# Store and move issues regrouped at the end of an attention and spectral-mixing kernel: 64-row stores on the Sync queue, three late row moves on Sync, two more wide jobs stored block by block

## The chip, the cores and the metric

The kernel runs on one core of one Trainium2 chip. The metric is the device time of one execution in microseconds (us), as a median over runs. A profile is of one execution; its clock starts at its own first instruction. To compare profiles I measure from one landmark, the start of ScalarE's copy of `yl`, the last thing that no edit here touches, and write such times as L+x.

## The reference, cut to what matters

Causal attention with decay over 8 batches, 8 heads, 576 positions, then spectral mixing and a gated output:

```python
x = attention(q, k, v, f)                 # 8 x 576 x 512 after joining heads
X = np.fft.rfft(x, axis=1)                # 64 modes are kept
Y[:, :64] = complex_matmul(X[:, :64], w_r, w_i)   # per mode a 512 x 512 matrix
y = np.fft.irfft(Y, n=576, axis=1)
u = x + y
out = u + np.maximum(u @ w_ch, 0.0)       # 9.44 MB, float32
```

## The kernel before

For some 400 us the kernel streams weights. The change is in what follows. When the last modes are done, their inverse-transform rows are computed for all batches into `yls[0]`, and small DMAs ("moves", 16 KB each) carry each batch's rows to where TensorE needs them in `yy`. The move of batch b is written (b,0) for the plain rows and (b,1) for the rows multiplied by `w_ch`.

```python
def emit_moves(yl, r0, b, t, eng):
    p0 = H4 * b
    ins = eng.dma_start(row_slot(b, t, r0, H4), yl[p0 : p0 + H4, t, :])
    if eng is nc.gpsimd:
        tc.keep_in_program_order(ins)
...
nc.scalar.copy(yls[0][:, 0, :], ply[:, :])          # the landmark L
emit_moves(yls[0], H2, 1, 0, nc.gpsimd)
run(terms(jobs[0], ps, 0, "y"))
...
nc.vector.tensor_copy(yls[0][:, 1, :], plw[:, :])
emit_moves(yls[0], H2, 1, 1, nc.gpsimd)
for b in range(2, B):
    for t in range(2):
        emit_moves(yls[0], H2, b, t, nc.gpsimd)
```

Then 20 jobs follow. In each, TensorE makes two PSUM tiles (`pu` = u, `pz` = u times `w_ch`), ScalarE copies `pu` out, VectorE does relu and add, and Sync or ScalarE stores the block:

```python
def emit_o(job, ps, u, o, pair, split=False):
    ...                                              # VectorE: relu and add
    if sb == 4:                                      # the 64-row job of a batch pair
        for h in range(2):
            eng = (nc.sync, nc.scalar)[h]
            eng.dma_start(out[b + h, 512:576, :], o[64 * h : 64 * h + 64, 0, :])
    elif not wide(job):
        nc.sync.dma_start(...)
    elif sb % 2 or n_wide < 2:                       # wide: one store for two jobs
        rs = slice(sb % 2 if n_wide < 2 else 0, sb % 2 + 1)
        ...
```

While TensorE waits for the last weights, it is kept busy with matmuls whose results are overwritten later:

```python
def fill(n):
    for k in range(n):
        rows = slice(k % 2, k % 2 + 1)
        run(*(terms(jobs[0], ps, t, "x")[rows] for t in range(2)), pin=True)

fill(4)                                              # 16 matmuls of 512 columns
```

The softmax here doesn't subtract the row's maximum and nothing guards it: scores larger than these inputs give would overflow.

## Time and profile before

| | before |
|---|---|
| time, median of 3 runs | 437.63 us (437.60 to 438.23) |
| profiled span | 436.5 us |
| last compute ends (VectorE, job 19) | 428.16, L+26.13 |
| end of the span | L+34.47 |
| output | 9.44 MB in the last 31 us |

The sliced page shows where the change plays. Each figure stands for a fortieth of the span, so only the last three or four of each line count:

```profile
DMA  8999999999999999999999999999999999994797
GB/s 175 236 235 237 239 235 238 235 211 237 233 215 237 226 223 237 211 237 234 214 237 211 211 212 211 211 211 212 211 212 211 211 211 211 211 211 84 273 341 276
```

The weights keep the DMA engines at 0.9 until slice 36. Then there is a gap (84 GB/s), in which the late rows are made and moved, and after it the output stores. GpSimd's timeline of this gap (start, length, what; in brackets how long it was idle and what ended that):

```profile
403.21 0.51 POOL L823 DMA_DIRECT2D yy<-yl  x1 [17.51 <-ACT yl L1070]
404.15 4.30 POOL L823 DMA_DIRECT2D yy<-yl  x9 [0.42 <-DVE yl L1074]
```

GpSimd issues (1,0) at L+1.18, 0.6 us after ScalarE's copy has ended, and (1,1) at L+2.12, 0.30 us after VectorE's copy.

### The profile page before, as it was taken

Reading aid. Unit: us, or ns where it says so; the run is one execution under the profiler, and the core shown is the slowest. Engines: PE = TensorE matmul, PEld = TensorE weight load, DVE = VectorE, ACT = ScalarE, POOL = GpSimd, SP = SyncE. Lnnn points to the kernel's source line nnn. Section 1 sums busy time; section 2 is a strip of 40 time slices with the busy share of each in tenths; the row PEclk is TensorE's granted clock in tenths of the full one; section 3 lists DMA queues with packets and bytes.
Section 4 is the critical chain, followed back from the end, with each engine's and each line's share of the span. In section 5 each row is a group of like instructions: output and inputs, shape, how many; then the busy total and the mean of one; then the engine's idle time right before and its main releaser. Section 6 shows DMA issues by size and latency. Waiting matters only on the chain.

```text
span 436.5 us, 12293 instructions
## 1 busy us (share of the span) xinstructions
PE 357.7 (82%) x5295; PEld 243.4 (56%) x5313; DVE 263.8 (60%) x658; ACT 224.7 (51%) x340; POOL 128.9 (30%) x202
## 2 busy tenths in 40 slices
PE   3787798999797886877877886999979978899881
PEld 2454666776675665565655665766644544454440
DVE  5797888877565564665666677333233645553892
ACT  2887489775444636436447282233424434542670
POOL 7333332423233233232332232332223232200500
PEclk9996899998766857758759597799999999989997
DMA  8999999999999999999999999999999999994797
GB/s 175 236 235 237 239 235 238 235 211 237 233 215 237 226 223 237 211 237 234 214 237 211 211 212 211 211 211 212 211 212 211 211 211 211 211 211 84 273 341 276
DMA packets 50981, 97.37 MB, mean 223 GB/s; under 512 B 3792, under 2 KB 12976, under 8 KB 50928
## 3 DMA queue, kind: packets, MB, share of 16 engines
q0 software_dynamic: 46688, 86.16, 100.7%
q1 hardware_dynamic: 3920, 9.91, 6.3%
q8 instruction: 41, 0.67, 0.6%
q10 hardware_dynamic: 320, 0.52, 0.5%
q14 instruction: 12, 0.10, 0.1%
HBM read 163.73 MB, written 9.44 MB: 397 GB/s over the span
## 4 chain that ended last, share of the span: by engine, by line
DMA 40%; PE 26%; ACT 10%; DVE 7%; issue 4%; POOL 0%; DVEq 0%; ACTq 0%
DMA wb<-in_moe_w_i_dram 39%; ACT E L576 7%; PE pav L614 6%; PE ps L569 5%; PE A L188 5%; PE tp L307 4%; ACT KT L320 2%; DVE QTs L322 2%; PE vp L541 2%; DVE os L1005 1%; PE px L657 1%; PE pz L828 1%; ACT VT L326 1%; PE px L682 1%; DVE E L591 1%
## 5 line engine op out<-in xcount | busy, mean ns | idle before, releaser
L576 ACT ACTIVATE E<-ps 128x1024 bf16<-128x1024 f32 (+1 forms) x128 | 101.4, 851 | 21.7 <-PE ps L569 11.3
L188 PE MATMUL A<-XT,wb 128*128 128x16 bf16 x1984 | 70.4, 181 | 13.6 <-DMA wb<-in_moe_w_i_dram 8.9
L188 PEld LDWEIGHTS <-wb 128*128 128x128 bf16 x1984 | 63.7, 99 | 27.3 <-issue 11.4
L93 POOL DMA_DIRECT2D wb<-in_moe_w_r_dram x64 | 42.4, 663 | 119.6 <-DMA wb<-in_moe_w_r_dram 21.9
L569 PE MATMUL ps<-QTs,KT 64*128 64x64 bf16 (+4 forms) x384 | 56.8, 316 | 19.6 <-ACT E L576 17.7
L93 POOL DMA_DIRECT2D wb<-in_moe_w_i_dram x64 | 42.3, 661 | 87.3 <-DMA wb<-in_moe_w_i_dram 43.9
L614 PE MATMUL pav<-va,E 128*128 128x65 bf16 (+1 forms) x1088 | 53.1, 205 | 3.2 <-DVE x_all L636 2.6
L614 PEld LDWEIGHTS <-E 128*128 128x128 bf16 (+1 forms) x1088 | 43.5, 111 | 18.4 <-issue 9.3
L591 DVE TENSOR_TENSOR E<-E,trimask 128x256 bf16<-128x256 bf16 (+2 forms) x128 | 36.9, 302 | 20.5 <-ACT E L576 20.2
L867 ACT CAST XW<-pxw 128x512 bf16<-128x512 f32 x36 | 20.8, 587 | 39.4 <-PE pxw L860 34.5
L326 ACT COPY VT<-tp 128x640 bf16<-128x640 bf16 (+1 forms) x32 | 23.2, 761 | 32.4 <-PE tp L307 32.4
L569 PEld LDWEIGHTS <-KT 64*128 64x128 bf16 x384 | 18.8, 97 | 32.5 <-issue 20.9
L860 PE MATMUL pxw<-wch,yy 128*128 128x512 bf16 x133 | 35.1, 398 | 1.3 <-issue 0.5
L910 ACT CAST XW<-pB 128x512 bf16<-128x512 f32 x36 | 21.0, 586 | 27.8 <-PE pB L828 27.7
L320 ACT COPY KT<-tp 128x640 bf16<-128x640 bf16 (+1 forms) x32 | 21.9, 748 | 25.9 <-PE tp L307 25.8
L909 DVE CAST x_all<-pA 128x512 bf16<-128x512 f32 x36 | 24.9, 692 | 14.0 <-PE pA L828 12.4
L322 DVE COPY QTs<-tp 128x640 bf16<-128x640 bf16 (+1 forms) x32 | 23.4, 767 | 14.3 <-PE tp L307 14.0
L636 DVE TENSOR_TENSOR x_all<-pav,rcp 128x384 bf16<-128x384 f32 x64 | 29.1, 455 | 0.9
L153 DVE TENSOR_TENSOR YTe<-A,Yacc 128x128 bf16<-128x128 f32 x16 | 5.9, 367 | 33.1 <-PE A L188 33.1
L828 PEld LDWEIGHTS <-ident_bf 64*64 64x64 bf16 (+1 forms) x348 | 15.8, 108 | 17.9 <-issue 8.9
L625 DVE RECIPROCAL rcp<-pav 128x6 f32<-128x6 f32 x64 | 12.1, 189 | 20.0 <-PE pav L614 19.4
L860 PEld LDWEIGHTS <-yy 128*128 128x128 bf16 x144 | 12.7, 101 | 15.2 <-DVE yy L854 4.6
(143 smaller groups left out, 622.2 us busy)
## 6 DMA issues: line engine op xcount, KB each, us to landing
wb<-in_moe_w_r_dram POOLq DMA_DIRECT2D x62, 512.0 KB, 16.9
wb<-in_moe_w_i_dram POOLq DMA_DIRECT2D x62, 512.0 KB, 17.8
stv<-in_v_dram POOLq DMA_DIRECT2D x10, 576.0 KB, 15.1
out_dram<-os SPq DMA_DIRECT2D x10, 512.0 KB, 5.0
stk<-in_k_dram POOLq DMA_DIRECT2D x11, 288.0 KB, 15.3
stq<-in_q_dram POOLq DMA_DIRECT2D x11, 288.0 KB, 15.3
wx<-in_v_dram POOLq DMA_DIRECT2D x5, 576.0 KB, 15.5
out_dram<-uo SPq DMA_DIRECT2D x3, 512.0 KB, 4.0
```

Source lines behind the costliest of these rows:

```text
L93: keep(nc.gpsimd.dma_start(dst, src))
L188: ins = nc.tensor.matmul(A[:, eb, mi, :], lhsT=w_of(mi, eb * 128), rhs=x_of(m), start=(i == 0), stop=(i == len(terms) - 1),)
L320: nc.scalar.copy(rows(KTs[pr % 2][:, :, 0:S]), tv)
L322: ins = nc.vector.tensor_copy(rows(QT[pr][:, :, :]), tv)
L326: nc.scalar.copy(rows(VTs[pr % 2][:, :, 0:S]), tv)
L569: nc.tensor.matmul(ps[:, b, o : o + n], lhsT=KTs[pr % 2][bs, h, jb * 128 : (jb + 1) * 128], rhs=QT[pr][bs, h, jb * 128 + c0 : jb * 128 + c ...
L576: nc.scalar.activation(E[:, :, piece * 512 : piece * 512 + w], ps[:, :, 0:w], ACT.Exp, scale=scale,)
L591: nc.vector.tensor_tensor(dg, dg, tr, ALU.mult)
L614: nc.tensor.matmul(pav[64 * half : 64 * half + w, slot, :], lhsT=E[:, b, c : c + (w - 1) * st + 1 : st], rhs=va[:, jb, b, :], start=(n == ...
L636: nc.vector.tensor_tensor(xo, pi, ri, ALU.mult)
L860: nc.tensor.matmul(pxw[:, :], lhsT=xT[:, eb, i * 128 : (i + 1) * 128], rhs=wch[:, eb, :], start=(eb == 0), stop=(eb == NDC - 1),)
L909: nc.vector.tensor_copy(xs, pA[:, :])
```

## The change

It has three parts. (1) The moves (1,0), (2,0) and (3,0) go to Sync, to shorten GpSimd's line-up. (2) All 64-row stores but the very last go to Sync alone, so that no store issue stands in ScalarE's queue and Sync's and ScalarE's rings don't mix. (3) Jobs 7 and 8 (the second half of the first four wide jobs) are stored one by one, sooner.

```diff
-            if eng is nc.gpsimd:
+            if eng is nc.gpsimd or r0 == H2:
                 tc.keep_in_program_order(ins)
...
-                        eng = (nc.sync, nc.scalar)[h]
+                        eng = nc.scalar if job is jobs[-1] and h else nc.sync
...
-                elif sb % 2 or n_wide < 2:
-                    rs = slice(sb % 2 if n_wide < 2 else 0, sb % 2 + 1)
+                elif sb % 2 or n_wide < 4:
+                    rs = slice(sb % 2 if n_wide < 4 else 0, sb % 2 + 1)
...
-        emit_moves(yls[0], H2, 1, 0, nc.gpsimd)
+        for b in (1, 2, 3):
+            emit_moves(yls[0], H2, b, 0, nc.sync)
...
-            for t in range(2):
+            for t in range(1 if b < 4 else 0, 2):
                 emit_moves(yls[0], H2, b, t, nc.gpsimd)
```

## The prediction

> **What bounds the kernel now.** I read the sliced page first (the last three of 40 slices are the only ones above 270 GB/s), then the chain of waits, then the timelines of VectorE and Sync, half-microsecond windows, and last the DMA queues of chosen stretches. The change touches nothing before about 402.6 us, so 34 us of a 436.5 us span are in play. These last microseconds are: spectral weights end, late rows `yl` are copied by small DMAs into `yy`, then PE, ACT and DVE make 20 blocks ("jobs"; I number them 0 to 19) and 9.44 MB go out. Jobs 0-3 are of batches 0 and 1, job 4 is their 64-row job, jobs 5-8 are the wide ones of batches 2 and 3, 9 the 64-row one, and so on.
>
> The chain of waits, as pieces in order of time (start, length, what):
>
> ```profile
> 404.15 1.44 POOL yy L823 x3
> 405.58 3.76 DMA yy<-yl
> 409.35 0.04 issue
> 409.39 0.40 PE pu L828 x2
> ...
> 410.29 0.70 DVE uo L1005
> 411.00 0.02 issue
> 411.02 0.57 ACTq L1013
> 411.59 0.04 issue
> 411.63 1.02 ACT us L1000
> ```
>
> See two delays: PE waits until 409.35 for the fourth move behind GpSimd's line-up (batch 3, t=0), and a 0.57 us store issue stands in ScalarE's queue before the evacuation of job 6. The VectorE timeline shows the second delay again, and what the same spot costs in the next batch pair:
>
> ```profile
> 412.67 3.48 DVE L1005 SCALAR_TENSOR_TENSOR os<-pz,us 128x1024 f32<-128x1024 f32 x3 [0.56 <-ACT us L1000]
> ...
> 418.38 3.48 DVE L1005 SCALAR_TENSOR_TENSOR os<-pz,us 128x1024 f32<-128x1024 f32 x3 [0.21 <-ACT us L1000]
> ```
>
> But the last compute (VectorE, job 19) ends near 428.16, and the span ends at 436.5. So the bound of the end is the store traffic. Sync's timeline and the windows (length, busy of PE PEld DVE ACT POOL, clock, DMA share, GB/s):
>
> ```profile
> 425.33 4.02 SPq L1026 DMA_DIRECT2D out_dram<-os  x4
> 429.44 1.76 SPq L1013 DMA_DIRECT2D out_dram<-uo  x1
> ```
>
> ```profile
> 416.50:417.00 0.50, 0.50 (x16) 0.35 (x12) 0.32 (x2) 0.09 (x1) 0.00 (x0) 1.00 0.10 37
> 417.00:417.50 0.50, 0.50 (x16) 0.29 (x9) 0.50 (x1) 0.17 (x1) 0.00 (x0) 1.00 1.02 401
> ...
> 427.50:428.00 0.50, 0.00 (x0) 0.00 (x0) 0.50 (x2) 0.00 (x0) 0.00 (x0) 1.00 1.02 414
> ```
>
> At 416.5 the engines run dry, because job 7's block is held until job 8's is done. Adding the half-microsecond windows backwards from 435.0, the last 2.36 MB (eight 128x1024 stores and job 19) start to flow at about 427.4, 2.1 us after their first store was issued at 425.33: by then there is a backlog, and time lost earlier in the store stream is never won back. Where is it lost? The DMA queues of three stretches, 417.0 to 418.5, 418.5 to 420.5 and 424.0 to 426.0 (q1 is Sync's ring, q10 ScalarE's):
>
> ```profile
> DMA packets 162, 0.60 MB, mean 401 GB/s; under 512 B 15, under 2 KB 15, under 8 KB 162
> ```
>
> ```profile
> DMA packets 191, 0.57 MB, mean 287 GB/s; under 512 B 20, under 2 KB 20, under 8 KB 190
> q1 hardware_dynamic: 121, 0.44, 65.9%
> q10 hardware_dynamic: 69, 0.12, 31.2%
> ```
>
> ```profile
> DMA packets 205, 0.61 MB, mean 304 GB/s; under 512 B 27, under 2 KB 27, under 8 KB 205
> q1 hardware_dynamic: 135, 0.49, 68.9%
> q10 hardware_dynamic: 70, 0.12, 30.8%
> ```
>
> While ScalarE's 64-row store is mixed with Sync's stream, the engines are as busy as ever but move 287 and 304 GB/s, not 401. (In 427.5 to 430.0, q1 alone, it is 419.) Q10 holds 0.12 MB for 31% of the busy time, q1 0.44 MB for 66%: 2.6 against 1.5 per cent per 10 KB.
>
> **What the Trainium skill says.** "DMA: Bandwidth & Descriptors", section "Issuing engines are not separate DMA queues": DMAs of all issuers run on the same 16 engines and interleave, and spreading the issue saves only sequencer time. The trace agrees that they interleave, and goes further: total rate falls by about a quarter while they do. "SBUF — State Buffer", section "Door 1: The DMA port swizzle": 64 partitions reach only 8 of the 16 ports, with an asymptote near 218 GB/s. That speaks against two 64-row stores in a row on one queue; in the trace Sync's own 64-row stores sit in windows of 303 and 332 GB/s (420.5 and 427.0), mixed with other stores, so no window isolates one. "DMA: Bandwidth & Descriptors", section "Measured", has smaller transfers at lower rates; the trace disagrees where they are queued back to back: from 414.0 to 416.0 q1 alone moved 256 KB stores with 2 KB rows at 395 GB/s, 5% under the wide ones.
>
> **Part 1: three moves to Sync.** GpSimd issues 14 moves at 0.484 us each. Before, the order is (batch 1, t=0), (1,1), (2,0), (2,1), (3,0): the first at 403.21, the next from 404.15, so (3,0) is issued at 404.15 + 3 x 0.484 = 405.6 and lands at 409.35. After, (1,0), (2,0), (3,0) go to Sync as soon as ScalarE's copy of `yl` ends (402.03 + 0.59 = 402.62). Sync's earlier moves took 0.588 us each, so they are issued by 404.4; even at Sync's median of 4.6 us to landing, measured under the weight stream, (3,0) is there by 408.4. Sync's first output store was at 404.70, so it isn't delayed. GpSimd's (2,1) and (3,1) come two places earlier too, landing near 409. PE had the four x-terms of job 5 done near 408.45 and then waited; its last two y-terms began at 409.39 and now begin near 408.8. **Gain 0.6 us** for jobs 4 and 5.
>
> **Part 2: 64-row stores on Sync.** Four ACT issues become one. (a) The issue at 411.02 goes: ScalarE can begin job 6 as soon as `pu` is there, and VectorE's 0.56 us wait falls to the 0.2 or so of the later pairs. **Gain 0.35 to 0.55 us** of compute. The issues at 416.79 and 422.49 (0.49, 0.47) end before the `pu` that ScalarE then waits for; worth nothing in compute. So compute ends about 1.0 us earlier, at 427.1. (b) The mixing of rings goes for jobs 4, 9 and 14: in each of two stretches of 2 us about 2 x (401 - 295)/401 = 0.5 us was lost; at job 4 (412.5 to 413.5 at 193 and 283 GB/s, where a late issue overlaps it) perhaps as much. Against this, 0.26 MB of 64-row stores in a row at some 320 GB/s takes 0.8 us, not 0.65: 0.15 us each.
>
> **Part 3: jobs 7 and 8 one by one.** Two 512 KB stores become four of 256 KB, the first two a job earlier (job 7 ended 1.2 us before 8). That fills the dry half-microsecond at 416.5 (0.45 us). Cost: 1.05 MB in 2 KB rows, 5% of 2.6 us, 0.13 us; two more Sync issues of 0.33 to 0.5 us, hidden.
>
> **Sum, as a ledger of the store stream after the change.** The first 2.1 MB (jobs 0-3), paced by compute, flow until 412.6 as now (413.0, less the late GpSimd moves). Then job 4: 0.26 MB, 0.8 us, 413.4. Jobs 5-8: 2.1 MB at 395, 5.3 us, 418.7. Job 9: 0.8, 419.5. Jobs 10-13: 2.1 MB at 410, 5.1 us, 424.6. Job 14: 0.8, 425.4. The last 2.36 MB take 7.2 us now (427.4 to 434.6), ScalarE's last 64-row store still among them, so they end at 432.6. Can compute feed it? With everything 1.0 us earlier, jobs 10 and 11 are issued at 418.6, 12 and 13 at 420.9, 15 and 16 at 424.3: with the 0.8 us from issue to flow seen at 416.19 to 417.0, the first of these is flowing at 419.4, just in time, the others with room. 434.6 - 432.6 = **2.0 us** less: 437.63 - 2.0 = **435.6 us**, 0.5% faster.
>
> **Rivals.** (1) Compute sets the gain: the stream is no shorter, it only starts earlier, so the 1.0 us of parts 1 and 2a comes through: 436.6. For it: near-equal rates, one batch pair of 2.36 MB per 5.7 us of compute is 414 GB/s. Against: the backlog of 2.1 us at 427.4. (2) The slow stretches come from the 64 rows (8 ports), not from two rings; then two in a row on Sync are as slow or slower and the end moves by 0.5 us at most: 437.1. For it: the skill's port table; q10's cost per byte. Against: the windows 420.5 and 427.0 with Sync's own 64 rows at 303 and 332, for half a microsecond, not two. (3) Sync as the only issuer becomes the bound: its issues already stretch from 0.33 to 1.76 us late in the stream, and more stores wait for a completion eight stores back. Then the gain is lost: 437.6 or 0.3 more. Against: [...]the engines stay at 410 GB/s. (4) The moves on Sync land late behind output stores, and PE waits as before: 0.6 us less gain.
>
> **Range and chances.** The ledger gives 435.6; if both ring mixing and gap filling pay in full and the tail too, 434.8; rival 1 gives 436.6, rival 2 437.1. I hold the ledger at 0.6, rival 1 at 0.2, the others together 0.2: range 434.8 to 436.9. Two per cent is 8.75 us, more than the whole drain after the last compute: faster 0.01, slower 0.01, same 0.98.
>
> **What would show it.** Right: no DMA piece of `yy<-yl` near 409 in the chain; VectorE's wait before job 6 at 0.2 or less; its last end near 427.1; no window under 350 GB/s between 413 and 425 with q10 present; no dry window at 416.5; the last 2.36 MB starting near 425.4. Wrong: two 64-row stores on q1 in a stretch under 250 GB/s; Sync's issues beginning over 1 us after VectorE's ends while the DMA share is below 0.9; PE still waiting for a move.

## The result, and the profile after

| | before | after |
|---|---|---|
| time, median of 6 runs each, same rounds | 438.31 us (437.6 to 439.0) | 440.22 us (439.71 to 441.63) |
| ratio of the fast runs, 95% interval | | 1.0052 (1.0030 to 1.0073) |
| profiled span | 436.5 | 438.0 |
| last compute ends | L+26.13 | L+28.57 |
| end of the span | L+34.47 | L+36.50 |

A ratio is the mean time of one kernel's fast runs over that of the other's in the same rounds, so it is not quite the ratio of the medians. The kernel is 1.9 us slower, where 2.0 us faster was predicted. It is within 2%, but outside the predicted range of 434.8 to 436.9.

The chain of waits of the kernel after (start, length, what) has a DMA piece where the one of before stood. It ends at L+5.86, 1.5 us earlier than that one (L+7.32), and is almost as long:

```profile
403.52 0.47 issue
403.99 3.34 DMA yy<-yl
407.33 0.04 issue
407.37 0.64 PE pz L828 x2
...
411.11 1.24 DVE uo L1005
```

The timeline of TensorE shows the wait, and that of GpSimd the issue:

```profile
407.37 0.64 PE L828 MATMUL pz<-yy,BIl 64*64 64x512 bf16 x2 [1.89 <-DMA yy<-yl]
```

```profile
403.99 5.29 POOL L823 DMA_DIRECT2D yy<-yl  x11 [18.99 <-ACT uo L1000]
```

The late move is now (1,1), for job 2. With (1,0) gone, it is the first move that GpSimd issues, at L+2.52 instead of L+2.12, and it takes 3.34 us where it took 1.6. TensorE stands still for 1.89 us. The matmuls after it take 0.64 us where the same pair took 0.40, because the clock is halved. Half-microsecond windows (length, busy time of PE, PEld, DVE, ACT, POOL, then clock, DMA share, GB/s):

```profile
407.50:408.00 0.50, 0.50 (x8) 0.29 (x9) 0.00 (x0) 0.00 (x0) 0.50 (x2) 0.50 0.97 352
...
410.00:410.50 0.50, 0.50 (x10) 0.32 (x9) 0.18 (x1) 0.00 (x0) 0.00 (x0) 0.50 0.03 6
...
421.00:421.50 0.50, 0.15 (x4) 0.00 (x0) 0.50 (x2) 0.42 (x2) 0.00 (x0) 1.00 1.04 295
421.50:422.00 0.50, 0.47 (x10) 0.26 (x11) 0.50 (x1) 0.50 (x1) 0.00 (x0) 1.00 0.26 66
422.00:422.50 0.50, 0.50 (x12) 0.38 (x10) 0.50 (x1) 0.23 (x1) 0.00 (x0) 1.00 0.57 139
```

At 410.0 the engines have nothing to store, because compute is late. From 421.0 the 64-row pair of job 9 goes out, now on one ring. Sync takes 1.49 us (420.10 to 421.59) to issue the second store of the pair; its packets begin near 422.1, behind a dry stretch, and from 421.5 to 423.0 the engines move 150 GB/s. VectorE's timeline tells how late compute is, and that one step of the prediction came true:

```profile
408.95 1.23 DVE L1005 SCALAR_TENSOR_TENSOR uo<-pz,uo 128x1024 f32<-128x1024 f32 x1 [2.80 <-PE pu L828]
...
414.55 3.49 DVE L1005 SCALAR_TENSOR_TENSOR os<-pz,us 128x1024 f32<-128x1024 f32 x3 [0.21 <-ACT us L1000]
```

The wait before job 6 was 0.56 us and is 0.21. But VectorE lost 2.80 us before job 2. Job 5 starts at L+11.65 where it was L+8.87, 2.8 us later; compute ends 2.4 us later and the span 2.0 us later. Of these 2.0 us, 1.4 are the last store, which lands at L+34.77 (before: L+33.38). The other 0.6 us come after it: from that landing to the end of the span it is 1.73 us where it was 1.09. Sync there goes through the completion waits of the stores one after another, and 7 of them are still to come when the last store lands, where it was 4. No run isolates this.

For a stretch that holds little but a 64-row pair (112 of its 120 data packets are 2 KB rows), 428.0 to 429.0 of the kernel after, the DMA queues were:

```profile
DMA packets 153, 0.26 MB, mean 262 GB/s; under 512 B 33, under 2 KB 33, under 8 KB 153
q1 hardware_dynamic: 153, 0.26, 90.7%
```

One ring, no mixing, 0.9 busy, and still 262 GB/s. In the packet records of the kernel after, the mean 2 KB packet took 99 to 160 ns in the half-microseconds in which 64-row pairs flow on Sync's ring, and 84 to 90 ns where 128-row stores do. Not every packet is slower: in this stretch the median is 84 ns, and one in ten took over 165. (The 137 to 169 ns of an expectation below are means of the last store, on ScalarE's ring.)

### The profile page after: what moved, and what is told of

Same layout as the page of the kernel before. It is cut to its first block, busy times and chain, and to the rows that moved or that the text cites. A ratio compares the mean times of both kernels' runs of the same rounds, so it can differ in the third digit from the quotient of the medians.

```text
span 438.0 us, 12298 instructions
## 1 busy us (share of the span) xinstructions
PE 358.8 (82%) x5295; PEld 244.1 (56%) x5313; DVE 263.4 (60%) x658; ACT 224.7 (51%) x340; POOL 127.2 (29%) x199
## 4 chain that ended last, share of the span: by engine, by line
DMA 51%; PE 21%; ACT 7%; DVE 6%; issue 3%; DVEq 0%; POOL 0%; ACTq 0%; POOLq 0%
DMA wb<-in_moe_w_i_dram 43%; DMA stk<-in_k_dram 7%; ACT E L576 5%; PE pav L614 4%; PE ps L569 4%; PE A L188 3%; PE tp L307 3%; PE pz L828 2%; DVE os L1005 1%; PE px L657 1%; ACT KT L320 1%; DVE QTs L322 1%; PE px L682 1%; PE pu L828 1%; PE vp L541 1%
```

## The experiments

Fifteen variants ran, each five rounds against the kernel before; all were correct. J5 is the start of VectorE's work for job 5, C the end of compute, both in us from L and read from one profile each, so they can differ from the runs behind the ratio.

| run | ratio, 95% interval | J5 | C |
|---|---|---|---|
| (before) | | 8.87 | 26.13 |
| (after) | 1.0052 (1.0030 to 1.0073) | 11.65 | 28.57 |
| moves_only | 1.0055 (1.0026 to 1.0085) | 11.97 | 28.96 |
| no_moves | 0.9991 (0.9970 to 1.0012) | 8.68 | 25.41 |
| sync64_only | 0.9978 (0.9960 to 0.9996) | 8.95 | 25.69 |
| single_only | 0.9994 (0.9976 to 1.0011) | 9.07 | 26.33 |
| b11_sync | 1.0036 (1.0009 to 1.0063) | 12.77 | 30.68 |
| b10_pool | 0.9984 (0.9966 to 1.0002) | 8.30 | 25.22 |
| warm | 1.0043 (1.0015 to 1.0071) | 12.29 | 29.21 |
| first64 | 0.9985 (0.9965 to 1.0005) | 9.18 | 25.97 |
| after_shift48 | 0.9994 (0.9975 to 1.0012) | 9.17 | 26.09 |
| before_shift16 | 0.9998 (0.9979 to 1.0018) | 9.47 | 26.47 |
| before_shift48 | 0.9987 (0.9970 to 1.0004) | 8.30 | 25.29 |
| first64_single_b10 | 0.9980 (0.9965 to 0.9995) | 8.29 | 25.28 |
| b11_shift48 | 0.9990 (0.9974 to 1.0007) | 8.59 | 25.51 |
| b10_shift48 | 0.9992 (0.9975 to 1.0008) | 8.30 | 25.21 |
| best_shift48 | 1.0000 (0.9987 to 1.0013) | 8.29 | 25.31 |

### The parts by themselves

`moves_only` is part 1 alone, `no_moves` parts 2 and 3, `sync64_only` part 2, `single_only` part 3; each is the kernel before with those hunks of the diff, the first and the last two being part 1, the second part 2, the third part 3.

> Part 1 alone (three moves on Sync). Theory A: the loss sits here. GpSimd's first move of batch 1, t=1, now comes after a pause of 19 us and its 16 packets meet the first output stores, so it lands near 407.3 instead of 405.6, PE idles about 1.9 us and then runs at half clock: expect 1.5 to 2.8 us slower than before (ratio 1.003 to 1.006), the wait of PE for yy near 407 and the half clock both present. Theory B (the stores of parts 2 and 3 cost the time, the late move is hidden by the store backlog): within 0.5 us of before.

> Parts 2 and 3 without part 1. Theory A: the moves arrive as in the kernel before, PE doesn't idle near 407, and the gain of the dropped ScalarE issue (0.35 us) and of the filled gap (0.3 to 0.5 us) shows: 0.3 to 1.2 us faster than before. Theory B: 64-row stores in a row on one ring[...] (137 to 169 ns for a 2 KB packet in the changed kernel, 84 elsewhere): 0.5 to 2 us slower than before.

> Part 2 alone. Prediction's step 2: mixing of two rings goes (0.5 us each time), less 0.15 us each for 64 rows in a row, and compute gains 0.35: 0.8 to 1.4 us faster. From the changed kernel's packet times I now expect that the two rows of halves cost as much alone as mixed: 0 to 0.5 us faster. Theory B: slower by 0.5 us or more.

> Part 3 alone. Fills the dry half-microsecond at 416.5: if the store backlog bounds the end, 0.3 to 0.5 us faster; if compute or the pair's wait later on bounds it, within 0.2 us; the dry window should be gone in either case.

Measured: 440.37, 437.61, 437.19 and 437.96 us, against 437.85 for the kernel before. **The whole loss is in part 1**: its run has the same wait for the same move (2.08 us) and the halved clock. The other parts gain a little or nothing. Part 2 brings the end of compute forward by 0.44 us (26.13 to 25.69). Where the store stream's share went, Sync's timeline of `no_moves` shows:

```profile
419.18 1.91 SPq L1013 DMA_DIRECT2D out_dram<-uo  x2
421.18 3.19 SPq L1026 DMA_DIRECT2D out_dram<-os  x4
```

VectorE had ended job 11 at 420.15, but its store is issued at 421.18, because Sync was still issuing the two 64-row stores. The DMA engines run dry meanwhile:

```profile
420.50:421.00 0.50, 0.50 (x14) 0.29 (x10) 0.50 (x1) 0.39 (x1) 0.00 (x0) 1.00 0.08 29
```

So two store issues in a row on one queue made a hole of 0.5 us that two queues had not made.

### Who should issue which move

In `b11_sync`, (1,1) goes to Sync too; in `b10_pool`, (1,0) goes back to GpSimd, as its first move.

```diff
 # b11_sync, on the kernel after
-        emit_moves(yls[0], H2, 1, 1, nc.gpsimd)
+        emit_moves(yls[0], H2, 1, 1, nc.sync)
 # b10_pool, on the kernel after
-        for b in (1, 2, 3):
+        emit_moves(yls[0], H2, 1, 0, nc.gpsimd)
+        for b in (2, 3):
             emit_moves(yls[0], H2, b, 0, nc.sync)
```

> The changed kernel with batch 1, t=1 moved by Sync too, in one queue ahead of the output stores. Theory A (GpSimd's move behind the output stores is the loss): it lands before job 2 needs it, PE's 1.9 us wait and the half clock go: 1.5 to 2.5 us faster than the changed kernel, so 0 to 1 us faster than the kernel before. Rival (any use of Sync for moves delays the output stores, and that is the loss): still 1.5 us or more slower than before.

> The changed kernel with batch 1, t=0 given back to GpSimd, which issues it before batch 1, t=1; Sync keeps (2,0) and (3,0). If the first issue after GpSimd's pause is what lags (0.70 us behind VectorE's end in the changed kernel, 0.30 in the kernel before, where it came second), (1,1) is issued 0.4 us earlier against its inputs and lands before the stores flow: as fast as b11_sync, 0 to 1 us faster than before. If the landing is late for another reason, the wait of 1.9 us stays and it is 1.5 us or more slower than before.

`b10_pool` did as expected: no wait for (1,1), job 5 at L+8.30, 437.56 us against 437.99. `b11_sync` missed. Issued by Sync, the move was as late as in the kernel after, and TensorE stood for 2.21 us. In its profile, the slowest of its six runs, the clock then stayed halved for 10.2 us, where it was 3.4 us in the kernel after; this goes with its late C. So "GpSimd's first move is slow" could not be the whole cause.

### Does the halved clock do it?

`warm` puts 16 matmuls that add zeros into TensorE's wait, on the kernel after:

```diff
+            elif n == 2:
+                run([zs[0]], [us[0]], pin=True)
+                for _ in range(8):
+                    for p, _w, src, _f in zs[0]:
+                        tc.keep_in_program_order(add(p, BIe[1][HS[0], 0:HM], src, False))
+                run(zs[1:], us[1:], pin=True)
```

> The changed kernel with 16 matmuls of zero weights, adding nothing, in PE's wait for the move (some 1.7 us of work). The move lands as late as in the changed kernel, but PE doesn't stand still. If the half clock from 407 to 410.5 is a result of the standstill and half the damage, the clock stays full and it is 0.8 to 1.5 us faster than the changed kernel, 0.5 to 1.5 us slower than before. If the clock is halved regardless, it is as slow as the changed kernel.

Measured: 439.72 us. The move came later still (4.14 us), 1.29 us of wait were left, and the clock was halved all the same from about 409.9. This run is inconclusive: it did not separate the standstill from the clock.

`first64` keeps ScalarE's 64-row stores except for job 4 (`eng = nc.scalar if b and h else nc.sync`, on the kernel before).

> Part 2 for job 4 alone; the later 64-row stores stay split over Sync and ScalarE. From sync64_only: compute gains 0.44 us there by the dropped issue at job 4, while the later pairs on Sync hold up the next store (issue times of 3.1 and 2.5 us for two) for nothing. So 0.4 to 1.0 us faster than before, at least as fast as sync64_only. If instead the unmixing of the rings is what sync64_only gains from, about 0.2 us faster only.

Measured: 437.78 us, no different from part 2 as a whole within the intervals.

### What held up the move

A DMA counts its semaphore up to 16. The Trainium skill, "DMA: Bandwidth & Descriptors", section "Why a DMA increments its semaphore by 16 and not by 1", says that for a GpSimd DMA all 16 DMA engines post one count each, and that only the full 16 means that the data has landed. The trace's semaphore records agree, and they show what the profile's one number of 3.34 us hides. The last column is the 16,384-byte packet of the instruction queue nearest in time:

| kernel | move | issued | 15th count | 16th count | instruction packet |
|---|---|---|---|---|---|
| before | (1,1) | 404.15 | 405.75 | 405.78 | 406.83 to 407.71 |
| before | (3,0) | 405.58 | 408.03 | 409.35 | 406.83 to 407.71 |
| after | (1,1) | 403.99 | 406.30 | 407.33 | 404.95 to 406.28 |
| b11_sync | (1,1) | 404.55 | 406.41 | 408.24 | 405.46 to 406.82 |
| before_shift16 | (1,0) | 403.76 | 405.39 | 406.94 | 404.83 to 405.83 |
| after_shift48 | (1,1) | 404.53 | 406.89 | 406.92 | 401.50 to 402.57 |
| b11_shift48 | (1,1) | 404.60 | 406.43 | 406.46 | 401.61 to 402.54 |

In the kernel after, fifteen engines were done at 406.30 and the sixteenth 1.03 us later. In the stretch 404.9 to 406.3 of that kernel the view of the queues lists, beside Sync's ring and GpSimd's, one packet of a third:

```profile
q1 hardware_dynamic: 140, 0.26, 50.2%
q0 software_dynamic: 38, 0.02, 10.7%
q8 instruction: 1, 0.02, 6.0%
```

It is 16,384 bytes and took 1.33 us. The skill, "Runtime: NRT & Kernel Launch", section "Instruction fetch mechanics", says that each engine's instruction memory is refilled in blocks of 16 KiB, 256 instructions, over a DMA queue of its sequencer's own, and that the cost is "mostly hidden". The trace agrees on the block: it holds 5295 matmuls and 5313 weight loads of TensorE, 41.4 blocks of 256, and this queue carried 41 packets (42 with 48 loads and matmuls more). That it is hidden was to be tested. The runs with a shift in their names move the fetch in time and leave the moves alone: the 16 filling matmuls are cut into four (or two) of fewer columns each, which adds 48 (or 16) weight loads and as many matmuls at about the same TensorE time.

```diff
-        fill(4)
+        fill(4, 4)      # each of 512 columns as 4 of 128; before_shift16: fill(4, 2)
```

> The kernel after with 48 more weight loads and matmuls in TensorE's queue, at about the same TensorE time: the 16 filling matmuls before the last but one mode group, whose results are overwritten, are cut into four of 128 columns each. Nothing of the moves changes, only where in time the 16,384-byte instruction fetches fall (they come about every 128 weight loads; in the kernel after one ran on one DMA engine from 404.95 to 406.28, over the move of batch 1, t=1, whose last completion count came at 407.33). Theory F (the fetch holds up the move): the fetch comes some 5 us earlier, the move lands near 405.7 to 406.0, no 3 us DMA piece in the chain, the clock isn't halved, compute ends near +26 of the copy of yl, time 437.2 to 438.0, ratio to before 0.998 to 1.001. Theory O (the move is late because it is GpSimd's first and starts 0.4 us later, into the first output stores; the early fetch is only a by-product of TensorE's wait): wait and time as in the kernel after, ratio 1.004 to 1.006.

> The kernel before with 16 more weight loads and matmuls ahead, by cutting the same 16 filling matmuls in two. Its fetch, at 4.80 us after the copy of yl, should come some 16 loads sooner, near 3.4 to 3.5 us after it, when the move of batch 1, t=1 is in flight (issued 404.15, complete 405.78 in the kernel before). Theory F: that move, or one behind it, is complete 1 to 2 us later, TensorE stands, ratio to before 1.003 to 1.006; if the move's packets on that engine are through before the fetch begins, which is possible because it starts 0.4 us sooner here than after the change, only part of it, 1.001 to 1.003. Theory O: as before, 0.999 to 1.001.

> The kernel before with the 48 additional weight loads and matmuls of the first run: a control for that edit, and a look at whether the fetch also causes the late landing of batch 3, t=0 (409.35 in the kernel before, with a fetch from 406.83 to 407.71). Theory F: the 3.76 us DMA piece that ends at 409.35 shrinks to 2 to 2.5 us, compute of job 5 begins up to 0.6 us earlier, ratio 0.997 to 0.9995. Theory O: nothing moves, 0.999 to 1.001.

`after_shift48`: **the loss is gone**, 437.89 us against 438.17, where the same kernel without the edit stood at 1.0052. The fifteenth and sixteenth count are 0.03 us apart. The kernel before with the same loads stands at 0.9987, so with the fetch out of the way on both sides the change is worth nothing that these intervals show. The wait and the clock:

```profile
406.96 0.40 PE L828 MATMUL pz<-yy,BIl 64*64 64x512 bf16 x2 [0.95 <-DMA yy<-yl]
```

```profile
407.50:408.00 0.50, 0.50 (x14) 0.32 (x8) 0.11 (x1) 0.12 (x1) 0.50 (x2) 1.00 0.63 211
```

`before_shift16` makes the fault appear in the kernel before. The fetch now falls on the first move, (1,0), whose sixteenth count comes 1.55 us after the fifteenth; TensorE waits where it had not waited:

```profile
406.98 0.40 PE L828 MATMUL pu<-yy,BIl 64*64 64x512 bf16 x2 [1.04 <-DMA yy<-yl]
```

It fell one move earlier than I had aimed. The clock stayed whole, job 5 came 0.6 us later than before, and the time did not move measurably (0.9998): here only the trace speaks for theory F, the ratio lies where theory O had it. `before_shift48` takes the fetch away from all of the early moves. The DMA piece that ends at 409.35 in the kernel before disappears and job 5 starts at L+8.30: with no change to any move, it has 0.57 of the 0.6 us that part 1 was to bring.

I looked at the 17 profiles together. In the 12 without the 48 loads the fetch falls among the moves issued after L, and some move's sixteenth count comes 1.0 to 1.95 us after its fifteenth. In the five with them the fetch is over by L+0.6 and no such gap is over 0.34 us.

For the miss of `b11_sync`, and for what GpSimd's order is worth by itself, the same 48 loads were put into those two variants:

> The kernel with batch 1, t=1 on Sync as well (its run missed: 1.0036, TensorE waiting 2.21 us), now with the 48 additional weight loads that put the instruction fetch elsewhere. Theory F (that miss was the fetch too): the move, issued about 2.5 us after the copy of yl begins, lands within 1.5 to 2.4 us, TensorE waits at most 0.9 us, the clock is not halved, ratio 0.997 to 1.000. Rival (a move issued this late lands late in any case, because the output stores have begun): wait over 1.3 us, clock halved, ratio 1.003.

> The kernel after with batch 1, t=0 left as GpSimd's first move, and with the 48 additional weight loads. If the fetch costs this variant nothing (its run showed no wait at the moves, 0.9984), nothing changes: 0.997 to 1.0. If the fetch held up other moves in it (three of GpSimd's had their last count 1.6 to 1.9 us behind the fifteenth), these come sooner: 0.996 to 0.998. In both, the wait at batch 1, t=1 stays under 0.4 us, which, beside the 0.95 us of the first run with 48 more loads, is what the order of GpSimd's moves alone is worth.

The profile of `b11_shift48` has TensorE wait this long, where `b11_sync` had 2.21 us:

```profile
406.50 0.40 PE L828 MATMUL pz<-yy,BIl 64*64 64x512 bf16 x2 [0.37 <-DMA yy<-yl]
```

So that miss had the same cause. `b10_shift48` has no wait for a move at all. The 0.95 us that `after_shift48` keeps is therefore what giving up (1,0) as GpSimd's first move costs. In time it is not to be seen (0.9992 and 0.9994).

### A better version

> The parts that earlier runs showed to help, together: 64-row stores on Sync for the first of the four 64-row jobs alone, the blocks of jobs 7 and 8 one by one, batch 1, t=0 left as GpSimd's first move, and t=0 of batches 2 and 3 on Sync. If the gains add (0.9985 for the first part, 0.9994 for the second, 0.9984 for the kernel after with GpSimd's first move given back): 0.996 to 0.998, 436.1 to 437.1. Rival: the end is paced by the last 2.36 MB of stores behind a compute that ends no earlier in any of these, and the gains do not add: 0.998 to 1.000.

> The kernel with Sync's 64-row stores for the first 64-row job alone, single blocks and GpSimd's first move given back (0.998), and the 48 additional weight loads. If the gains add: 0.9965 to 0.998, 436.4 to 437.1. If the store stream sets the end whatever the compute does: as without the loads, 0.998 to 0.9995.

`first64_single_b10` is the kernel after with the edits of `first64` and `b10_pool`; `best_shift48` adds the 48 loads to it.

The first ran at 437.53 us against 438.17, ratio 0.9980: faster than the kernel before by 0.2%, and no faster than part 2 alone (0.9978). With the additional weight loads the gains did not add: 438.30 us against 437.99, ratio 1.0000, though compute ends at L+25.31, 0.8 us before that of the kernel before. In its profile the stores did not take this back: the last one landed at L+32.16, 1.2 us sooner than in the kernel before. But from there to the end of the span it is 1.86 us, where it was 1.09, and L itself came 0.4 us later, 402.45 for 402.03.

## Why the prediction was right or wrong

**Part 1, the step that failed.** The text says of GpSimd's queue only that "(2,1) and (3,1) come two places earlier too, landing near 409". It did not ask which move becomes the first, and which job needs that one. It is (1,1), whose first matmul runs at L+3.8 in the kernel before and for which TensorE stands from L+4.0 on in the kernel after; it is issued 0.4 us later and lands later. Alone that is 0.95 us of wait and nothing in the time. The rest came from what no line of the argument had: an instruction fetch that fell on this move. Shown is that moving the fetch, with the moves unchanged, takes the late sixteenth count away (in all five variants with the 48 loads) and puts it on another move in `before_shift16`. Argued only is that both sit on the same DMA engine: the packet records don't name the engine. In the table the late sixteenth count comes 1.0 to 1.6 us after the fetch has ended, which I take for that engine's backlog, and which no run isolates. Open is why the fetch comes at L+3.4 to L+3.5 in the four runs that have (1,0) on Sync and no added loads, and at L+4.6 to L+4.8 in the others without added loads, though the change touches none of TensorE's instructions. So the early fetch may belong to the change and need not be chance.

What part 1 aimed at came about, but not for the reason given, and that is luck. Sync's (3,0) landed at 405.04, even sooner than the 408.4 predicted, and with (1,0) given back job 5 starts 0.57 us earlier, for 0.6 predicted. But `before_shift48` shows the delay of (3,0) for what it was: a fetch, not GpSimd's line-up, which TensorE does not wait for at all in that run.

**The halved clock** was not in the prediction. Waits of 0.37, 0.95 and 1.04 us left the clock whole; waits of 1.29, 1.89, 2.08 and 2.21 us were followed by half clock. That is a coincidence in seven runs, not a test. The two together, fetch and clock, are worth 1.0052 − 0.9994 = 0.58%, 2.5 us.

**Part 2a was right**: 0.44 us of compute for 0.35 to 0.55.

**Part 2b was mis-sized, and rival 2 was nearer.** The term is "0.26 MB of 64-row stores in a row at some 320 GB/s takes 0.8 us". Alone on one ring they ran at 262 GB/s, 1.0 us, for job 14, and at job 9, with the wait for the second issue, at 150. The slow windows were those of the 64 rows more than those of two rings. Rival 3 came true beside it: in `no_moves` Sync's 64-row issues, 1.91 us for two, held the next store back by 1.0 us.

**Part 3** filled the dry window at its own place, and another dry stretch came later; 0.3 us predicted, 0.9994 with an interval of 0.9976 to 1.0011 measured.

**The sum.** Parts 2 and 3 without part 1 gave 0.9991, 0.4 us, where the ledger's 2.0 us less the 0.6 us of part 1 leave 1.4. The ledger let each gain shorten the stream and ended with the stream. With the fetch away (`after_shift48`) the last store did land sooner, at L+31.93 against L+32.81 in `before_shift48`, 0.9 us for the 2.0 predicted; but 1.75 us then passed to the end of the span, against 1.09. The variants whose compute ended 0.4 to 0.9 us earlier had ratios from 0.9978 to 1.0000, with no order by the end of compute; all of them with changed moves or stores have 1.3 to 1.9 us behind the last landing. These are single profiles, and L alone differs by up to 2 us between them. Rival 4 asked whether a move on Sync would land late; the wait came, but behind a move that had stayed on GpSimd. All three listed signs of failure came true: TensorE still waiting for a move and 64-row stores at 150 GB/s (421.5 to 423.0, the dry stretch between them included) in the kernel after, and Sync's issue over 1 us behind VectorE in the run without part 1. Two slips in the prediction change no sum: (3,0) is GpSimd's fifth move, not the fourth, and the last 2.36 MB are four wide stores and job 19, not eight. And the table of "Measured" that it says the trace disagrees with is of loads issued by GpSimd; the 395 GB/s of queued stores from Sync do not contradict it. The chances, 0.98 for within 2%, held.

## What to carry to other kernels

When moves or loads are shared out anew between queues, ask which transfer becomes the first and which engine waits for it, not only which ones come sooner. If a small DMA on the critical path is late although the engines aren't full, look at its sixteenth completion count and at the instruction queue: a block of instructions may stand on one DMA engine, and some added or removed instructions much earlier move it. A change of half a per cent can hang on such an alignment, so test it with a shift of the instruction stream before believing either sign.

## What the Trainium skill lacked or had wrong

- "Runtime: NRT & Kernel Launch", section "Instruction fetch mechanics", calls the fetch of a 16 KiB block mostly hidden. Its block size agrees with 41 packets for 10,608 recorded matmuls and weight loads. What it lacks is that a fetch, 0.88 to 1.60 us of one DMA packet here, can come with another DMA's last count 1.0 to 1.95 us late, and that this, with the halved clock behind it, cost 2.5 us in the kernel after.
- "DMA: Bandwidth & Descriptors", section "Why a DMA increments its semaphore by 16 and not by 1": agrees, fifteen counts by 406.30 and the sixteenth at 407.33 in the kernel after. No page says that the gap between the two is the sign by which to tell a straggling engine from a slow transfer.
- "SBUF — State Buffer", section "Door 1: The DMA port swizzle": its asymptote of 218 GB/s for 64 partitions was the better guide than my windows, but two 64-row stores of opposite halves, one after the other on one ring, moved 262 GB/s here (428.0 to 429.0 of the kernel after). That they overlap in part is my guess.
- "TensorE: Matmul & The Clock Gate", section "What's actually happening", has the two clock states, which agree (0.50 and 1.00), and an idle window of about 3.4 us. Here a standstill of 1.89 us was followed by half clock, and one of 1.04 us was not.
- No page has what a 64-row store costs its issuing queue when several are outstanding: 1.91 us for two in `no_moves`, with a dry DMA window of 29 GB/s behind them.
